# One more column group of the signal spectrum kept on chip, with a new order, new homes, banks and engines

## The chip, the cores and the metric

The kernel runs on one NeuronCore of a Trainium2 chip. The metric is the device time in microseconds of one execution of the whole program. An execution's time contains the profiled span and a little around it.

## The reference

Two independent parts share the kernel, each 2048 positions by 448 columns, and their outputs stand side by side. All data are bf16.

```python
# A: linear attention with a learned feature map, 16 heads of 28
pq, pk = q @ w_phi, k @ w_phi                  # per head
phi = concat(softmax(p), softmax(-p))          # for q and for k
kv, z = phi_k^T v, sum_s phi_k
a = ((phi_q kv) / (phi_q z + 1e-6)) @ wo
# B: a state-space convolution, 448 columns of 256 states
K[d, l] = Re sum_n C[d,n] exp(dt*A[d,n] * l) dt*B[d,n]
y = irfft(rfft(pad(u)) * rfft(pad(K)))[:2048] + u * Dskip
```

## The kernel before

**Part B** is a convolution by spectra. Its 448 columns are cut into eight chunks of 56 (112 with both halves of the states), and two chunks make one of four column groups (`GROUPS`). For each chunk: the *phases* are matmuls of a table of multiples with the log of the state's step (`dampings`, `rotations`); ACT makes exponentials and sines of them out of PSUM; DVE multiplies them (`damp`); a chain of five doublings (`hi_tables`) makes the coarse powers, each of two products and one addition; `build_k` multiplies the coarse and fine tables on PE into the kernel's values, which a copy brings from PSUM to SBUF. For each group: `scatter_k` moves these values by 36 small DMAs to the partitions where the transform wants them; `kernel_spectrum` transforms them on PE; `conv_group` multiplies the signal's spectrum `SU` and the kernel's spectrum `SK` on DVE, complex, as four big products of 3584 elements with three additions and some subtractions; `inverse` transforms back and stores.

The signal's spectrum is made early, for all groups, in `signal_spectrum`: 32 matmul blocks, each copied out of PSUM. The groups in `PARK` send theirs to DRAM (`SUd`) and read them back (`load_su`) before their convolution:

```python
if gi in PARK:
    sg = sb("sg", [128, 4, 112])
    copy(sg[:, :, :], (p, lambda t: t[:, :, :]))
    dma(["SP", "POOL"], SUd[gi][:, b, cp, st_, :, c0:c0 + 112], sg[:, :, :], ...)
else:
    copy(SUs[gi][:, b, cp, st_, :, c0:c0 + 112], (p, lambda t: t[:, :, :]))
```

**Part A** runs as 16 key tiles (projection, two exponentials, a DMA transpose, sums, one reciprocal, one product, accumulation in PSUM) and four query quarters (exponentials, reciprocals, four numerators, an addition of the two softmax halves, a transpose, the output projection and a store). Its tiles fill the gaps of part B.

**What sets the order.** The program first records 1366 units of work and runs none. Each unit lists the engines that may do it. `Plan.run` then issues them in the order of a table: each token of `ORDER` is a unit's number and the letter of its engine (P for PE, D for DVE, A for ACT, G for POOL, S for SP). Each engine keeps this order. `HOMES` gives every SBUF tile its byte address (one big tile `sbuf`, so all operands bear that name in the profile), and `BANKS` gives every PSUM tile its bank. A tile can lie where another one is done, and then waits for it.

Two kinds of unit can change engine with a meaning for this case. `copy` (L342) runs on ACT or DVE. An addition, `total`, runs on DVE (L379) or as a DMA issued by POOL that adds on the way (L381):

```python
if e == "DVE":
    nc.vector.tensor_tensor(out=dst, in0=dst, in1=t2, op=ALU.add)
else:
    nc.gpsimd.dma_start(out=view(dst), in_=view(t2), accum_op=ALU.add, ...)
```

Plain DMAs (L366) may go to SP or POOL, DMA transposes (L371) to SP. All matmuls are L351, products and subtractions on DVE L322, activations L332.

Of the kernel before, what the change touches and what calls it, by code (L numbers as in the profile page):

```python
# [30 lines left out]
PARK = [1, 2, 3]  # L31
# [60 lines left out]
0S 2A 3A 4S 5S 7S 28G 43P 44A 45D 42D 6S 46P 52A 49A 47P 30G 53D 71P 54A 72A 55D 73P 38G 51A 74A 50A 8S 140G 75P 77D  # L92
37S 48A 80D 76P 79D 17S 78D 57A 82D 56A 58D 81D 59D 649P 654A 61A 25S 657A 60A 655A 646P 648A 656A 39S 62D 650A 139G
141S 40S 69A 64A 142G 651A 143D 63D 144D 653A 95D 652A 88D 94D 89D 189S 190G 639P 19S 636P 65A 22S 41G 68A 191D 151P
647A 168P 640A 21S 18S 642A 638A 20S 118P 119A 225P 645A 226A 145P 637A 70D 169A 112P 192D 104D 210P 66D 23S 644A 24S
126P 643A 127A 641A 216P 211A 186P 102A 676D 113A 96G 180P 90G 219P 67D 92D 187A 217A 207P 114P 146A 218G 91D 97D 115A
93G 100A 122P 123A 213P 159P 98D 152A 214A 208A 103D 107A 680D 12S 124P 156P 116P 199P 234P 117A 200A 125A 34G 120P
675D 101D 235A 682D 677D 181A 121A 10S 9S 678D 681D 248P 105A 270P 272A 109D 259P 99G 660D 273A 262A 659D 171P 679D
201P 13S 220A 221G 250A 202A 195P 236G 196A 661D 174P 11S 170S 108D 261A 110A 172A 175A 106D 147P 212G 292P 294A 157A
303P 160A 295A 158G 183P 184A 658S 663D 662D 281P 283A 111D 237P 240A 14S 711D 148A 710D 712G 35G 203S 29G 165P 306A  # L100
664D 284A 166A 209G 239A 305A 149P 251A 204P 336P 150A 338A 153P 193P 188S 205A 194A 690P 154A 339A 665D 215G 666D
667D 669D 668D 670D 672D 671D 176S 696A 709S 714D 197P 687P 691A 155S 700P 673D 713D 688A 715D 27S 716D 693A 717D 198A
718D 297S 674G 685P 683P 689A 692A 695A 719D 694A 720D 708A 701A 707A 731D 721D 26S 1S 703A 161G 697P 698A 727D 699A
31G 725G 705A 173S 704A 314P 83P 722D 228P 206S 723D 684A 84A 129S 724G 686A 177P 702A 726D 229A 178A 179G 706A 85A
# [81 lines left out]
BANKS = "2246060577464565566424057205213025364344223317722252233000363614704367562041217134315736107506766202\  # L186
# [50 lines left out]
class Bytes:  # L237
# [32 lines left out]
def kernel(  # L270
# [752 lines left out]
    for gi, (c0, n) in enumerate(GROUPS):  # L1023
# [7 lines left out]
        scatter_k(gi, Ts)  # L1031
        if gi in PARK:
            load_su(gi)
# [33 lines left out]
```

## Time and profile before

| | before |
|---|---|
| median of 3 runs | 277.54 us (274.92 to 279.04) |
| the profiled execution | 275.77 us, span 274.0 us |
| PE busy | 233.8 us (85%) |
| DVE busy | 247.1 us (90%), 334 instructions |
| ACT busy | 235.0 us (86%), 414 instructions |
| POOL busy | 97.3 us (36%) |
| DMA moved | 39.10 MB |
| HBM read, written | 13.18 MB, 6.42 MB |

Busy time is time in which an engine works; neighbours on one engine overlap by about a tenth of a microsecond, so a group's busy time is less than its count by its mean. A group's line shows engine, operation, output and input with shapes, count, busy time, mean nanoseconds of one, and the engine's idle time just ahead with what ended it. The chain of waits follows the work that ended last back from the end. Three engines are almost equally full here, so a share of the span alone doesn't tell which of them sets the time; where one waits for another does.

### The profile page before, as it was taken

Reading aid. Unit: us, or ns where it says so; the run is one execution under the profiler, and the core shown is the slowest. Engines: PE = TensorE matmul, PEld = TensorE weight load, DVE = VectorE, ACT = ScalarE, POOL = GpSimd, SP = SyncE. Lnnn points to the kernel's source line nnn. Section 1 sums busy time; section 2 is a strip of 40 time slices with the busy share of each in tenths; the row PEclk is TensorE's granted clock in tenths of the full one; section 3 lists DMA queues with packets and bytes.
Section 4 is the critical chain, followed back from the end, with each engine's and each line's share of the span. In section 5 each row is a group of like instructions: output and inputs, shape, how many; then the busy total and the mean of one; then the engine's idle time right before and its main releaser. Section 6 shows DMA issues by size and latency. Waiting matters only on the chain.

```text
span 274.0 us, 10764 instructions
## 1 busy us (share of the span) xinstructions
PE 233.8 (85%) x4620; PEld 199.8 (73%) x4620; DVE 247.1 (90%) x334; ACT 235.0 (86%) x414; POOL 97.3 (36%) x169
## 2 busy tenths in 40 slices
PE   3825788999896797698999998979997998998994
PEld 3724686789786476376669977979895998788964
DVE  1699989999999899799899999997999989999891
ACT  3999999999999998996998999998969992756551
POOL 2400221260113330302942362176757210657450
PEclk9995999999999999999999999998999999999998
DMA  7996996455548797981431699399987797125764
GB/s 188 327 362 119 173 208 118 140 153 129 130 110 126 130 165 115 122 93 22 63 75 19 198 237 203 52 250 164 142 135 105 187 219 138 11 16 93 177 178 113
DMA packets 66969, 39.10 MB, mean 143 GB/s; under 512 B 53372, under 2 KB 62954, under 8 KB 66666
## 3 DMA queue, kind: packets, MB, share of 16 engines
q1 hardware_dynamic: 57914, 23.22, 40.7%
q0 software_dynamic: 8400, 14.94, 28.5%
q8 instruction: 36, 0.59, 1.0%
q10 hardware_dynamic: 608, 0.26, 0.3%
q14 instruction: 11, 0.09, 0.1%
HBM read 13.18 MB, written 6.42 MB: 72 GB/s over the span
## 4 chain that ended last, share of the span: by engine, by line
PE 31%; ACT 30%; DVE 19%; issue 8%; DMA 6%; SPq 4%; POOL 0%; ACTq 0%; DVEq 0%; POOLq 0%
PE psum L351 31%; ACT sbuf L332 20%; DVE sbuf L322 16%; ACT sbuf L342 5%; DMA sbuf<-sbuf 4%; SPq L366 4%; ACT L332 4%; ACT sbuf L337 1%; DVE sbuf L379 1%; DMA sbuf<-in_B_A_re_dram 1%; DVE sbuf L326 1%; DVE sbuf L545 0%; POOL sbuf L381 0%; DVE sbuf L342 0%; DVE sbuf L801 0%
## 5 line engine op out<-in xcount | busy, mean ns | idle before, releaser
L351 PE MATMUL psum<-sbuf 128*128 128x112 bf16 (+7 forms) x4620 | 233.8, 247 | 36.4 <-ACT sbuf L332 15.8
L351 PEld LDWEIGHTS <-sbuf 128*128 128x128 bf16 (+4 forms) x4620 | 199.8, 117 | 70.2 <-issue 38.5
L322 DVE TENSOR_TENSOR sbuf<-sbuf 128x896 bf16<-128x896 bf16 (+6 forms) x232 | 191.6, 873 | 13.8 <-ACT sbuf L332 9.2
L332 ACT ACTIVATE sbuf<-psum 128x448 bf16<-128x448 f32 (+4 forms) x221 | 138.5, 759 | 2.4 <-PE psum L351 2.0
L342 ACT CAST sbuf<-psum 128x448 bf16<-128x448 f32 (+3 forms) x167 | 84.1, 591 | 25.5 <-PE psum L351 25.0
L366 POOL DMA_DIRECT2D sbuf<-sbuf x68 | 46.8, 821 | 37.8 <-ACT sbuf L342 22.6
L381 POOL DMA_DIRECT2D sbuf<-sbuf x25 | 24.2, 994 | 66.1 <-DVE sbuf L322 47.4
L379 DVE TENSOR_TENSOR sbuf<-sbuf 128x896 bf16<-128x896 bf16 (+1 forms) x43 | 35.4, 833 | 0.4
L332 ACT ACT_TABLE_LOAD x17 | 21.8, 1283 | 5.0 <-PE psum L351 3.1
L366 POOL DMA_DIRECT2D out_dram<-sbuf x17 | 11.2, 693 | 17.0 <-ACT sbuf L342 17.0
L366 POOL DMA_DIRECT2D SUd<-sbuf x13 | 8.2, 649 | 23.8 <-ACT sbuf L342 23.8
L322 DVE TENSOR_TENSOR sbuf<-psum,sbuf 128x896 f32<-128x896 f32 (+4 forms) x14 | 8.8, 654 | 5.1 <-ACT sbuf L332 3.8
L731 POOL MEMSET sbuf<- 128x112 bf16 x16 | 3.7, 328 | 10.6 <-PE psum L351 10.4
L801 DVE RECIPROCAL sbuf<-psum 128x32 bf16<-128x32 f32 x16 | 5.3, 342 | 0.2 <-PE psum L351 0.2
L337 ACT CAST sbuf<-sbuf 128x1792 bf16<-128x1792 f32 x3 | 5.4, 1788 | 0.0
L337 ACT CAST sbuf<-psum 128x896 bf16<-128x896 f32 x2 | 1.8, 909 | 2.8 <-PE psum L351 2.8
L326 DVE SCALAR_TENSOR_TENSOR sbuf<-sbuf 128x64 f32<-128x64 f32 (+2 forms) x7 | 4.1, 590 | 0.0
L844 DVE RECIPROCAL sbuf<-psum 128x128 f32<-128x128 f32 x4 | 3.8, 949 | 0.2 <-PE psum L351 0.2
L366 POOL DMA_DIRECT2D sbuf<-SUd x2 | 1.7, 826 | 6.3 <-DVE sbuf L322 6.3
L342 DVE CAST sbuf<-psum 128x448 bf16<-128x448 f32 (+1 forms) x5 | 2.9, 583 | 0.9 <-PE psum L351 0.9
L332 ACT ACTIVATE sbuf<-sbuf 128x1792 f32<-128x1792 f32 x2 | 3.5, 1757 | 0.0
L847 DVE RECIPROCAL sbuf<-sbuf 128x64 f32<-128x64 f32 x4 | 2.1, 535 | 1.4 <-DMA sbuf<-sbuf 1.4
(21 smaller groups left out, 18.6 us busy)
## 6 DMA issues: line engine op xcount, KB each, us to landing
sbuf<-sbuf POOLq DMA_DIRECT2D x20, 224.0 KB, 4.9
sbuf<-sbuf POOLq DMA_DIRECT2D x8, 448.0 KB, 6.0
sbuf<-const SPq DMA_DIRECT2D x4, 640.0 KB
sbuf<-const SPq DMA_DIRECT2D x2, 1024.0 KB
out_dram<-sbuf POOLq DMA_DIRECT2D x17, 112.0 KB, 3.0
sbuf<-SUd SPq DMA_DIRECT2D x4, 448.0 KB
out_dram<-sbuf SPq DMA_DIRECT2D x15, 112.0 KB
SUd<-sbuf POOLq DMA_DIRECT2D x13, 112.0 KB, 2.7
```

Source lines behind the costliest of these rows:

```text
L322: lambda e: nc.vector.tensor_tensor(out=at(out_), in0=at(a), in1=at(b), op=op), [whose(a), whose(b)], [out_])
L326: lambda e: nc.vector.scalar_tensor_tensor(out=at(out_), in0=at(a), scalar=sc, in1=at(b), op0=op0, op1=op1),
L332: lambda e: nc.scalar.activation(at(out_), at(a), func, scale=scale, bias=bias), [whose(a)], [out_],
L337: plan.add({"ACT": 0.039 + sbuf + count(out_) * 0.8333e-3}, lambda e: nc.scalar.copy(at(out_), at(a)), [whose(a)], [out_])
L342: lambda e: (nc.scalar.copy if e == "ACT" else nc.vector.tensor_copy)(at(out_), at(a)), [whose(a)], [out_])
L351: nc.tensor.matmul(out_, lhsT=lhsT, rhs=rhs, start=start, stop=stop, **kw)
L366: plan.add({e: own[e] for e in engs}, lambda e: QUEUES[e].dma_start(out=out_, in_=in_, **kw), r, w, load=pieces / 16000 * max(11, 7.5 + 0. ...
L379: nc.vector.tensor_tensor(out=dst, in0=dst, in1=t2, op=ALU.add)
L381: nc.gpsimd.dma_start(out=view(dst), in_=view(t2), accum_op=ALU.add, max_dma_last_dim=3584)
L731: pool(0.5, lambda en: [nc.gpsimd.memset(w[:, c, ZERO, :], float(np.sqrt(0.5))) for c in range(2)], [], [w[:, 0, ZERO, :], w[:, 1, ZERO, :]])
L801: nc.vector.reciprocal(rk, pz.t)
L844: plan.add({"DVE": 0.868}, lambda e: nc.vector.reciprocal(rz[:, :, :, :], at(ndv(1))), [pz], [rz[:, :, :, :]])
```

## The change

`PARK` becomes `[2, 3]`: the second column group's signal spectrum (group 1) is written from PSUM straight into its tile in SBUF, where it stays until its convolution. Eight stores of 112 KB into DRAM and two loads of 448 KB leave the program, which has 1356 units now. `ORDER`, `HOMES` and `BANKS` are new throughout. No function changes.

```diff
-PARK = [1, 2, 3]
+PARK = [2, 3]
...
 ORDER = """
-0S 2A 3A 4S 5S 7S 28G 43P 44A 45D 42D 6S 46P 52A 49A 47P 30G 53D 71P 54A 72A 55D 73P 38G 51A 74A 50A 8S 140G 75P 77D
+666G 2A 42D 28G 0S 43P 44A 30G 5S 45D 71P 72A 3S 46P 52A 53D 4S 47P 54A 7S 55D 6S 73P 74A 49A 8S 140G 75P 80D 77D 76P
...
-BANKS = "2246060577464565566424057205213025364344223317722252233000363614704367562041217134315736107506766202\
+BANKS = "2023464076166131424510655700506365110224555076460201600227243512070746105235560102275202012037042042\
```

Counted over the whole table, what each engine is given:

| | before | after |
|---|---|---|
| copies out of PSUM: ACT, DVE | 167, 5 | 160, 12 |
| additions: DVE, POOL | 43, 25 | 39, 29 |
| plain DMAs: SP, POOL, ACT | 141, 106, 2 | 121, 117, 1 |
| DMA transposes: SP | 48 | 48 |
| ACT table loads | 17 | 17 |

Matmuls, activations and products are the same in number and size. Line numbers after are one lower than before.

Three places of the order. First DVE, in the damping of the sixth chunk (rows of 448, 1792 and 2688 elements, the last dimension 112), among the first query quarter's reciprocals and products. Before:

```order
L322 TENSOR_TENSOR sbuf<-sbuf 128x4x112 x2
L844 RECIPROCAL sbuf<-psum 128x128
L322 TENSOR_TENSOR sbuf<-sbuf 128x16x112
L322 TENSOR_TENSOR sbuf<-psum,sbuf 128x128
L322 TENSOR_TENSOR sbuf<-sbuf 128x1792 x2
L326 SCALAR_TENSOR_TENSOR sbuf<-sbuf 128x64
L322 TENSOR_TENSOR sbuf<-sbuf 128x2688
L847 RECIPROCAL sbuf<-sbuf 128x64
```

After:

```order
L321 TENSOR_TENSOR sbuf<-sbuf 128x4x112
L341 CAST sbuf<-psum 128x448
L321 TENSOR_TENSOR sbuf<-sbuf 128x896
L321 TENSOR_TENSOR sbuf<-sbuf 128x4x112
L843 RECIPROCAL sbuf<-psum 128x128
L341 CAST sbuf<-psum 128x448
L321 TENSOR_TENSOR sbuf<-sbuf 128x896
L321 TENSOR_TENSOR sbuf<-psum,sbuf 128x128
L321 TENSOR_TENSOR sbuf<-sbuf 128x4x112
L321 TENSOR_TENSOR sbuf<-sbuf 128x1792 x2
L341 CAST sbuf<-psum 128x2x224
```

Three copies out of PSUM (two query numerators and one of the first group's kernel spectrum) now stand in DVE's row, which before held none here.

Second POOL, from the additions of the query quarters to the first stores of results. `SUd_58` and `SUd_59` are the third and fourth group's parked spectrum before, `SUd_57` is the third group's after. Before:

```order
L381 DMA sbuf<-sbuf 128x2x448
L366 DMA sbuf<-sbuf 32x1x28
L366 DMA sbuf<-SUd_59 128x1792
L366 DMA sbuf<-SUd_58 128x1792
L381 DMA sbuf<-sbuf 128x1792
L731 MEMSET sbuf 128x112 x2
L366 DMA out_dram<-sbuf 512x1x112 x2
```

After:

```order
L380 DMA sbuf<-sbuf 128x1792
L365 DMA sbuf<-SUd_57 128x1792
L365 DMA sbuf<-sbuf 32x1x28
L365 DMA sbuf<-sbuf 4x1x28
L365 DMA sbuf<-in_A_wo_dram 64x1x448
L365 DMA sbuf<-sbuf 4x1x28
L365 DMA sbuf<-SUd_57 128x1792
L380 DMA sbuf<-sbuf 128x896
L365 DMA out_dram<-sbuf 512x1x112
L380 DMA sbuf<-sbuf 128x1792
L365 DMA sbuf<-sbuf 4x1x28
```

Both additions of the second group's convolution (128x1792) are DMAs now, and the second of them stands behind a store of the second group's first output half; between them is the eighth chunk's last table addition (128x896), which was on DVE.

Third DVE, from the end of the last damping to the third group's convolution: the addition of a query quarter (128x2x448) and what follows. Before:

```order
L379 TENSOR_TENSOR sbuf<-sbuf 128x2x448
L847 RECIPROCAL sbuf<-sbuf 128x64
L322 TENSOR_TENSOR sbuf<-sbuf 4x112
L322 TENSOR_TENSOR sbuf<-sbuf 128x3584
L379 TENSOR_TENSOR sbuf<-sbuf 128x1792
L379 TENSOR_TENSOR sbuf<-sbuf 128x896
L322 TENSOR_TENSOR sbuf<-sbuf 128x896 x3
```

After:

```order
L378 TENSOR_TENSOR sbuf<-sbuf 128x2x448
L321 TENSOR_TENSOR sbuf<-sbuf 128x3584
L341 CAST sbuf<-psum 128x49x7
L321 TENSOR_TENSOR sbuf<-sbuf 128x896 x2
L378 TENSOR_TENSOR sbuf<-sbuf 128x896
L321 TENSOR_TENSOR sbuf<-sbuf 128x896 x2
L378 TENSOR_TENSOR sbuf<-sbuf 128x896
L321 TENSOR_TENSOR sbuf<-sbuf 128x896
L341 CAST sbuf<-psum 128x448
```

The addition of 1792 elements is gone from here (POOL has it). The copy of one of the last two kernel builds (128x49x7), which ACT made before, stands behind the third group's first product (128x3584); the second of the two subtractions of 896 behind it is the second group's and needs both additions.

More of the change, by code (lines that the diff above doesn't have):

```diff
@@ L152 @@
-1180G 557A 616S 472G 1359D 1347A 558S 1348S 1360P 1363P 612S 1364A 1361D 1362S 1365S
-"""
-HOMES = {"PID": [62432], "H": [155776], "AT": [50432], "TH": [38592], "PW128": [42176], "PW256": [56704], "PW512":
-         [98720], "P64": [104608], "ident": [8384], "negid": [104096], "ones": [99168], "LT": [87552], "half":
-         [108576], "HZ": [34304], "IDX": [205600], "xT": [177376, 141792, 34944, 94848], "WpQ": [19072], "WpK":
[3 rows of a table removed]
-         "rawCre": [164352], "rawCim": [166528], "rawBre": [87680], "rawBim": [196576], "ldt": [141280], "dt":
[11 rows of a table removed]
-         12736, 99168, 50368, 173056], "EKT": [148640, 171200, 47552, 86176, 173056, 104352, 49536, 166528, 55808,
[3 rows of a table removed]
-         [22656, 99168, 177280, 56832, 34944, 170112, 70432, 82272], "oT_": [191680, 55808, 54784, 193280, 53760,
[9 rows of a table removed]
```

129 lines of the change are left out of this document (68 added, 61 removed), and 51 rows, old and new, of the table HOMES.

## The prediction

> **What bounds the kernel now.** I read the busy line first, then the chain of waits by engine, a table by stretches of the span, the groups by shape, the waits, and the chain in order of time.
>
> ```profile
> span 274.0 us, 10764 instructions
> PE 233.8 (85%) x4620; PEld 199.8 (73%) x4620; DVE 247.1 (90%) x334; ACT 235.0 (86%) x414; POOL 97.3 (36%) x169
> PE 31%; ACT 30%; DVE 19%; issue 8%; DMA 6%; SPq 4%; POOL 0%; ACTq 0%; DVEq 0%; POOLq 0%
> ```
>
> Three engines are nearly full and the chain passes between them; no queue of DMAs holds more than 4% of it. The table by stretches (us, then busy us and instructions of PE, weight loads, DVE, ACT, POOL, clock, DMA share, GB/s) says where each is fullest:
>
> ```profile
> 40.00:80.00 40.00, 36.64 (x714) 30.96 (x714) 39.01 (x52) 39.94 (x75) 9.31 (x20) 1.00 0.59 143
> 80.00:130.00 50.00, 41.04 (x953) 32.24 (x946) 47.05 (x71) 45.85 (x80) 11.32 (x21) 1.00 0.72 106
> 130.00:205.00 75.00, 71.52 (x1516) 62.37 (x1516) 70.83 (x107) 69.94 (x127) 39.05 (x62) 0.98 0.69 140
> 205.00:235.00 30.00, 26.97 (x582) 23.70 (x580) 28.31 (x40) 23.77 (x44) 9.19 (x16) 1.00 0.77 151
> 235.00:274.00 39.00, 33.75 (x532) 28.47 (x529) 31.45 (x40) 20.18 (x43) 19.77 (x33) 0.98 0.50 103
> ```
>
> From 40 to 80 ACT has no gap (0.06 us), from 130 to 205 PE idles 3.5 of 75. DVE idles 0.99, 2.95, 4.17 and 1.69 us in the first four stretches, 9.8 in all: that is all a better order can win on DVE between 40 and 235. Whom DVE waits for stands in the waits (us in total, times, longest) and in its first rows in order of time:
>
> ```profile
> DVE sbuf L322 <- ACT sbuf L332: 13.0, 11, 3.8
> ...
> PE psum L351 <- ACT sbuf L342: 4.4, 8, 0.9
> ...
> 3.16 0.63 DVE L322 TENSOR_TENSOR sbuf<-sbuf 112x448 bf16<-112x448 bf16 x1 [3.16 <-ACT sbuf L332]
> ...
> 7.71 2.09 DVE L322 TENSOR_TENSOR sbuf<-psum,sbuf 128x896 bf16<-128x896 f32 x2 [3.82 <-ACT sbuf L332]
> ...
> 36.45 4.10 DVE L322 TENSOR_TENSOR sbuf<-sbuf 128x1792 bf16<-128x1792 bf16 x4 [1.31 <-DMA sbuf<-sbuf]
> ```
>
> Of the 13.0 us behind ACT's exponentials and sines, 3.16 + 3.82 are the lead-in; 6.0 lie inside, at the start of the chunks' dampings. The chain in order of time shows the end:
>
> ```profile
> 217.55 2.63 ACT sbuf L332 x3
> ...
> 222.53 4.10 DVE sbuf L322 x4
> 226.63 0.55 DVE sbuf L379
> ...
> 227.22 4.73 PE psum L351 x152
> ...
> 235.41 0.70 SPq L366
> ...
> 247.40 3.49 DMA sbuf<-sbuf
> ...
> 251.03 2.73 PE psum L351 x52
> ...
> 254.40 2.04 DVE sbuf L322
> ...
> 270.27 0.53 ACT sbuf L342
> ```
>
> The last chunk's damping exponentials (217.55) let DVE finish the damping (to 226.63) and add up the last table (0.55); then come the last two kernel builds on PE, their scatter on SP (235.41 to 247.40), the last kernel spectrum, the last convolution (254.40) and the inverse. Whatever makes those exponentials end earlier moves all of this, if DVE keeps up.
>
> **The change part by part.** The rows by shape (busy us, mean ns, idle before):
>
> ```profile
> L342 ACT CAST sbuf<-psum 128x448 bf16<-128x448 f32 x147 | 75.0, 599 | 16.4 <-PE psum L351 15.9
> L322 DVE TENSOR_TENSOR sbuf<-sbuf 128x1792 bf16<-128x1792 bf16 x68 | 71.8, 1083 | 4.2 <-ACT sbuf L332 2.0 <-DMA sbuf<-sbuf 1.3 <-ACT sbuf L342 0.3
> L322 DVE TENSOR_TENSOR sbuf<-sbuf 128x896 bf16<-128x896 bf16 x88 | 50.6, 612 | 0.4
> L322 DVE TENSOR_TENSOR sbuf<-sbuf 128x2688 bf16<-128x2688 bf16 x16 | 24.7, 1554 | 0.6
> L322 DVE TENSOR_TENSOR sbuf<-sbuf 128x3584 bf16<-128x3584 bf16 x12 | 24.1, 2016 | 1.4 <-ACT sbuf L342 1.3
> L381 POOL DMA_DIRECT2D sbuf<-sbuf x25 | 24.2, 994 | 66.1 <-DVE sbuf L322 47.4 <-ACT sbuf L332 9.8 <-PE psum L351 5.2
> L379 DVE TENSOR_TENSOR sbuf<-sbuf 128x1792 bf16<-128x1792 bf16 x20 | 21.5, 1080 | 0.3
> L379 DVE TENSOR_TENSOR sbuf<-sbuf 128x896 bf16<-128x896 bf16 x23 | 14.2, 619 | 0.2
> L322 DVE TENSOR_TENSOR sbuf<-sbuf 128x448 bf16<-128x448 bf16 x32 | 11.5, 381 | 4.0 <-ACT sbuf L332 4.0
> L366 POOL DMA_DIRECT2D SUd<-sbuf x13 | 8.2, 649 | 23.8 <-ACT sbuf L342 23.8
> L342 DVE CAST sbuf<-psum 128x448 bf16<-128x448 f32 x3 | 1.9, 620 | 0.9 <-PE psum L351 0.9
> ```
>
> *Parking removed.* Eight stores of 112 KB and two loads of 448 KB go: ten issues on SP and POOL. POOL's ran 649 ns, behind waits of 23.8 us for ACT's copies, and POOL has 0% of the chain; SP's share lies in the last scatter alone, where no parking stands. The copies out of PSUM stay (they now write the resident tile), so no engine work goes. I take 0: cover is POOL at 36%. Were a load of the parked group what its convolution waited for, it would gain; but those products' whole group (128x3584) waited 1.4 us, for copies. Bounds: -1.3 to 0.
>
> *Engines chosen anew.* Net seven copies of 448 columns go from ACT to DVE (eleven copies go there and four come back; one each way is of 343 columns), and net four additions go from DVE to a DMA that adds, issued by POOL (three of 1792, one of 896 elements). ACT: -7 x 0.599 = -4.2 us. DVE: 7 x 0.620 - 3 x 1.080 - 0.619 = +0.5 us. PE's matmuls are the same. So DVE's own work, the largest, is not less.
>
> *ACT's lighter queue.* Seven copies fewer stand ahead of what DVE waits for. Bounds: 0, and the 6.0 us that DVE waits inside (4.0 in the row of 448 elements, 2.0 in that of 1792). Those waits can't shrink by more than ACT gets earlier, 4.2; nearly all of the seven stand ahead of the last damping or ease the queue up to it. I take -4.0, the end nearest to the 4.2 of the rows.
>
> *Copies in DVE's queue.* A copy waits in order for its matmul, with everything on DVE behind it. The order shows three such in the damping of the sixth chunk; behind them products and reciprocals of the query stage are queued, and the copies and transposes of those quarters wait for them. The trace has three such copies of 448 columns, which waited 0.9 us together, all of it at the last of them. For the ten moved in: 0 to 9; I take +0.5, near to the two that didn't wait, since DVE is behind PE through most of the span.
>
> *Additions moved to POOL.* The DMA rows (median us from issue to landing):
>
> ```profile
> sbuf<-sbuf POOLq DMA_DIRECT2D x20, 224.0 KB, 4.9
> sbuf<-sbuf POOLq DMA_DIRECT2D x8, 448.0 KB, 6.0
> ```
>
> The last table's addition leaves the chain (0.55 at 226.63). Its DMA is queued on POOL behind a load of parked spectrum, and six dampings are on DVE behind its products (two each of 448, 1792 and 2688 elements: 2 x 0.38 + 2 x 1.08 + 2 x 1.55 = 6.0 us) against 4.9: covered, gain at most 0.55. The second column group's addition is worse placed. In the changed order both halves are DMAs and the second stands on POOL behind an output store that waits for an ACT copy eleven instructions past the last damping exponential. Eleven at 0.51 (75.0 over 147) are 5.6; plus 0.65 for the store's issue and 6.0 to land: 12.3 us after that exponential. DVE asks for it after five dampings (5.6), a product of 3584, a multiplication of 1792, an addition and a subtraction of 896, and two small ones put at 0.9 (2.0 + 1.1 + 0.6 + 0.6 + 0.9 = 5.2): at 10.8. It would wait 1.5, with the third group's finishing steps, the reciprocals of the last query quarter and the third group's second products queued behind, and PE's inverse matmuls waiting for those. What idle DVE has between 226.6 and 254.4 (1.3 us in the 128x3584 row, behind copies) would take up part. Bounds 0 to +4 (an addition's landing took up to 8.5 us, below); I take +1.0.
>
> The Trainium skill's page "DMA: Bandwidth & Descriptors", section "Anatomy of one DMA", fits a POOL-issued transfer as 2.0 us plus bytes over 436 GB/s. For 448 KB that makes 3.1, an estimate by that page, where this trace has 6.0; by it the wait vanishes and the sum would be -3.0. The measured row decides.
>
> *The early additions.* The chain has this at the first state tables:
>
> ```profile
> 27.30 0.67 POOL sbuf L381
> 27.97 8.46 DMA sbuf<-sbuf
> ```
>
> DVE waited 1.31 us for it at 36.45. In the new order there stand between the product and its use two signal sums of 1792 and one operation of 1.08 us fewer, and two dampings of 448 and one of 1792 more: -2 x 1.08 - 1.08 + 2 x 0.38 + 1.08 = -1.4 us of cover, so the wait grows by 1.4. It lies ahead of the stretch where ACT is full, and DVE's chunks wait for ACT behind it; I take 0, and +1.4 if ACT's lead makes DVE the late one there.
>
> *Scatter and end.* SP still issues 18 and POOL 14 transfers into the last kernel tile: 0. The last stores are reordered: 0, -0.5 to +0.8. Homes and banks make waits that this trace can't show: bounds -1 to +2 (the largest waits inside for a buffer or a bank, PE behind ACT's copies, were 0.9 each), taken at 0.
>
> **Sum.** +0.5 - 4.0 + 0.5 + 1.0 = -2.0 us. Against the profiled execution, 275.77 us (span 274.0 and 1.77 around it), that is 273.8. That execution lies 1.77 under the median of the runs, 277.54, which spread from 274.92 to 279.04; against the median the forecast is **275.5**.
>
> **Rivals.** *A, the order closes most gaps.* Of DVE's 9.8 us idle between 40 and 235 some 80% go: -7.8 + 0.5 = -7.3, so 270.2. For it: the gaps are many and small. Against it: three engines are at 85 to 90%, so each gap closed on one must fit two others.
>
> *B, PE holds the middle.* From 130 to 205 PE idles 3.5 us in 75, with the same matmuls after. An ACT that is ahead then only waits, and just what is won before 130 can stay: DVE's 2.95 of idle from 80 to 130, of which I give a third. 277.54 - 1.0 + 0.5 + 0.5 + 1.0 = 278.5. Against it: PE enters that stretch when ACT lets it, so it may start it earlier.
>
> *C, slower: DVE waits in its own queue for PSUM.* Each of the ten copies moved in waits as the one at the end did, 0.9 us, instead of near 0. Half of that, 0.5 each, gives 277.54 + 0.5 - 4.0 + 5 + 1.0 = 280.0; all of it 284.0. It turns the change slower from 0.25 us each. For it: the order puts three of them right in a damping. Against it: ACT's copies as a group waited 15.9 us for PE over 147, 0.1 each.
>
> *D, slower POOL.* Fifteen more DMAs are issued by POOL, 20 fewer by SP. The additions took 994 ns each on POOL with DVE 90% busy. The Trainium skill's page "SBUF — State Buffer", section "Who interferes with whom", says that POOL can be locked out from writing descriptors while DVE holds the port that they share, and gives about 3.1 us in place of 0.62 for such a DMA. As a mechanism here: the addition before the third group lands two us later, the wait above is 3.5 and not 1.5: 277.5. The 994 ns speak against more.
>
> **How the numbers follow.** Chances: forecast 0.36, A 0.20, B 0.24, C 0.14, D 0.06. 2% is 5.5 us, about what a measurement can tell here. Faster by more: A and a little of the forecast's low side, 0.22. Slower by more (over 283.1): the upper half of C and the worst of the homes' waits, 0.11. Within: 0.67. The range goes from just under A, 269.5, to between C's two values, 282.0.
>
> **What would show it.** Right: copies on ACT down by 4 us, DVE's busy time within 1 us of 247.1, its waits behind ACT's exponentials well under 13.0, the last scatter starting some 2 us before 235. B: PE still near 95% from 130 to 205 and ACT with new waits for PE there. C: waits of DVE copies for PE of over 3 us in all. The addition: a DVE wait for a DMA of 1 to 2 us shortly after the last damping. Wrong in kind: a wait for a parked load, or a new one of several us in the first 40.

## The result and the profile after

The changed kernel takes 293.23 us (median; 291.49 to 301.18), beside 277.08 us of the kernel before on the same chip: a ratio of 1.056, 95% interval 1.045 to 1.068. It is slower by 16 us, where 275.5 was forecast and the range ended at 282.0. The profiled execution took 291.49 us, span 289.6. (Some executions are disturbed and longer; the ratios and, below, the median times of the experiments leave these out.)

First the busy line and the chain by engine, from the page of the kernel after:

```profile
span 289.6 us, 10761 instructions
PE 234.6 (81%) x4620; PEld 199.2 (69%) x4620; DVE 247.4 (85%) x337; ACT 233.1 (80%) x407; POOL 107.5 (37%) x184
PE 28%; ACT 13%; DVE 13%; issue 7%; DMA 6%; SPq 2%; POOL 0%; DVEq 0%; ACTq 0%; POOLq 0%
```

The three engines do the same work as before: PE +0.8 us, DVE +0.3, ACT -1.9. So the 15.6 us more of span are idle time on all three. Next, how much each engine worked in the first 40 us, as the sums of ten stretches of 4 us. Before:

```profile
sum 40.00, PE 23.89 PEld 22.05 DVE 30.42 ACT 35.35 POOL 8.66; mean PE 2.39 PEld 2.20 DVE 3.04 ACT 3.54 POOL 0.87
```

After:

```profile
sum 40.00, PE 17.55 PEld 16.29 DVE 21.04 ACT 28.92 POOL 5.96; mean PE 1.75 PEld 1.63 DVE 2.10 ACT 2.89 POOL 0.60
```

DVE is 9.4 us behind, PE and ACT 6.3 and 6.4, before the first chunk is done. DVE's instructions in order of time show where it stood still (start, us, what, in brackets the idle time ahead and what ended it). Before:

```profile
16.09 3.02 DVE L322 TENSOR_TENSOR sbuf<-sbuf 128x1792 bf16<-128x1792 f32 x2
...
22.57 9.03 DVE L322 TENSOR_TENSOR sbuf<-sbuf 128x1792 bf16<-128x1792 bf16 x8
```

After:

```profile
16.63 1.08 DVE L325 SCALAR_TENSOR_TENSOR sbuf<-sbuf 128x896 bf16<-128x896 f32 x1
27.95 5.96 DVE L321 TENSOR_TENSOR sbuf<-sbuf 128x1792 bf16<-128x1792 bf16 x4 [10.24 <-DMA sbuf<-in_B_u_dram,sbuf]
```

After, the sums of the signal's second half stand at the head of DVE's row, and they need a gathered (indirect) load that is late. Before, the products of the first sine tables (`cs16`, `cs48`) and their like stand there. The load itself is in the groups of DMA issues (last number: median us from issue to landing). Before:

```profile
sbuf<-in_B_u_dram,sbuf POOLq DMA_INDIRECT x2, 9.0
```

After:

```profile
sbuf<-in_B_u_dram,sbuf POOLq DMA_INDIRECT x2, 17.1
```

PE has the same fault, and passes it on to ACT. PE's matmuls in order of time, before:

```profile
15.23 0.95 PE L351 MATMUL psum<-sbuf 128*128 128x112 bf16 x16 [0.66 <-DVE sbuf L322]
23.91 4.14 PE L351 MATMUL psum<-sbuf 128*128 128x112 bf16 x52 [7.73 <-ACT sbuf L332]
```

After:

```profile
13.77 1.73 PE L350 MATMUL psum<-sbuf 128*128 128x112 bf16 x32 [1.01 <-DVE sbuf L321]
30.10 6.08 PE L350 MATMUL psum<-sbuf 128*128 128x112 bf16 x93 [14.60 <-DVE sbuf L321]
```

ACT's first damping exponentials (896 elements wide before, 448 after), before:

```profile
27.60 2.16 ACT L332 ACTIVATE sbuf<-psum 128x896 bf16<-128x896 f32 x3
```

After:

```profile
27.99 1.28 ACT L331 ACT_TABLE_LOAD   x1
33.93 0.98 ACT L331 ACTIVATE sbuf<-psum 128x448 bf16<-128x448 f32 x2 [4.66 <-PE psum L350]
```

After, PE made two blocks of the rotations' phases (32 matmuls from 13.77) and then stood for 14.60 us: the first signal blocks are next in its row, and the first damping's phases, which need only the early tables, are behind them. Before, PE stood here too, for 7.73 us, but for ACT, which was at work all that time; after, ACT itself runs dry. Its first damping exponentials start at 33.93 instead of 27.60.

Does the early delay reach the end? The table follows six steps that both kernels have, in us from the span's start (found by their units in each engine's row). The last two columns are experiments, below.

| | before | after | rows moved (e2) | also homes (e3) |
|---|---|---|---|---|
| ACT's first damping exponentials | 27.6 | 33.9 | 28.7 | 29.2 |
| first doubling's last product ends | 27.7 | 40.5 | 31.5 | 27.7 |
| second chunk's damping ends | 79.2 | 91.4 | 82.9 | 83.3 |
| eighth chunk's damping ends | 226.6 | 239.4 | 231.8 | 233.8 |
| last kernel build ends | 234.0 | 246.7 | 238.4 | 240.6 |
| last group's first product | 254.4 | 269.3 | 262.1 | 262.8 |
| span | 274.0 | 289.6 | 282.4 | 283.0 |

It does: 12.8 us at 40, 12.2 at 91, 12.7 at 247, then 2.9 more behind the last build.

### The profile page after: what moved, and what is told of

Its sections match the earlier page's. It is cut to its first block, busy times and chain, and to the rows that moved or that the text cites. A ratio compares the mean times of both kernels' runs of the same rounds, so it can differ in the third digit from the quotient of the medians.

```text
span 289.6 us, 10761 instructions
## 1 busy us (share of the span) xinstructions
PE 234.6 (81%) x4620; PEld 199.2 (69%) x4620; DVE 247.4 (85%) x337; ACT 233.1 (80%) x407; POOL 107.5 (37%) x184
## 4 chain that ended last, share of the span: by engine, by line
PE 28%; ACT 13%; DVE 13%; issue 7%; DMA 6%; SPq 2%; POOL 0%; DVEq 0%; ACTq 0%; POOLq 0%
PE psum L350 28%; DVE sbuf L321 11%; ACT sbuf L331 9%; DMA sbuf<-sbuf 6%; ACT sbuf L341 3%; SPq L370 2%; ACT L331 1%; DVE sbuf L843 1%; DVE sbuf L341 0%; DVE sbuf L378 0%; POOL sbuf L365 0%; DVE sbuf L846 0%; DVE sbuf L800 0%; DVE sbuf L325 0%; DVEq L321 0%
## 5 line engine op out<-in xcount | busy, mean ns | idle before, releaser
L350 PE MATMUL psum<-sbuf 128*128 128x112 bf16 (+7 forms) x4620 | 234.6, 247 | 51.1 <-DVE sbuf L321 17.1
L321 DVE TENSOR_TENSOR sbuf<-sbuf 128x896 bf16<-128x896 bf16 (+9 forms) x232 | 190.9, 875 | 20.5 <-DMA sbuf<-in_B_u_dram,sbuf 10.2
L341 ACT CAST sbuf<-psum 128x448 bf16<-128x448 f32 (+3 forms) x160 | 81.9, 601 | 30.2 <-PE psum L350 28.3
L380 POOL DMA_DIRECT2D sbuf<-sbuf x29 | 27.9, 973 | 97.2 <-DVE sbuf L321 50.7
L365 POOL DMA_DIRECT2D sbuf<-sbuf x72 | 49.4, 775 | 22.1 <-ACT sbuf L341 15.4
L378 DVE TENSOR_TENSOR sbuf<-sbuf 128x896 bf16<-128x896 bf16 (+1 forms) x39 | 31.7, 818 | 0.5
L365 POOL DMA_DIRECT2D out_dram<-sbuf x23 | 16.1, 773 | 20.0 <-ACT sbuf L341 17.6
L365 POOL DMA_DIRECT2D SUd<-sbuf x11 | 7.2, 715 | 16.0 <-ACT sbuf L341 16.0
L341 DVE CAST sbuf<-psum 128x448 bf16<-128x448 f32 (+1 forms) x12 | 7.2, 603 | 3.9 <-PE psum L350 3.9
L336 ACT COPY sbuf<-psum 128x896 f32<-128x896 f32 x2 | 1.8, 905 | 4.5 <-PE psum L350 4.5
L636 POOL COPY sbuf<-sbuf 1x2 bf16<-1x2 bf16 x6 | 0.9, 174 | 7.5 <-DMA sbuf<-in_B_A_re_dram 4.2
L365 POOL DMA_DIRECT2D sbuf<-const x4 | 3.2, 802 | 0.0
```

Source lines behind the costliest of these rows:

```text
L321: lambda e: nc.vector.tensor_tensor(out=at(out_), in0=at(a), in1=at(b), op=op), [whose(a), whose(b)], [out_])
L336: plan.add({"ACT": 0.039 + sbuf + count(out_) * 0.8333e-3}, lambda e: nc.scalar.copy(at(out_), at(a)), [whose(a)], [out_])
L341: lambda e: (nc.scalar.copy if e == "ACT" else nc.vector.tensor_copy)(at(out_), at(a)), [whose(a)], [out_])
L350: nc.tensor.matmul(out_, lhsT=lhsT, rhs=rhs, start=start, stop=stop, **kw)
L365: plan.add({e: own[e] for e in engs}, lambda e: QUEUES[e].dma_start(out=out_, in_=in_, **kw), r, w, load=pieces / 16000 * max(11, 7.5 + 0. ...
```

## The experiments

Theories. *The rows*: work that needs the late load stands ahead of work that doesn't, on DVE, PE and ACT. *The landing*: the load is late because of what is issued ahead of it. *The homes*: tables wait for addresses that the signal's tiles still hold. *The engines and the tail*: the new engines of copies and additions, and more work behind the last build. *The parking*: keeping the spectrum in SBUF is itself a loss or a gain. Edits of the order are shown as one engine's row; a token is a unit.

**e1_loads: the load of the first half ahead of the weight transposes.** 185 and 141 on SP are the direct loads of the two halves, 17 to 20 the transposes of part A's weights, 25 a table.

```diff
 SP   185S
-25S 18S 20S 141S 19S 17S
+25S 141S 18S 20S 19S 17S
```

> The changed kernel with one edit in SP's row alone: the two transposes of weights that stand ahead of the load of the first signal half now stand behind it. Theory L (the gathered load lands 17.0 us after its issue, 9.0 before, because the transposes' small packets run beside it): it lands about 9 us after its issue, near 20.3 us, DVE's wait for it falls from 10.2 to 2 to 3 us, and the time falls by about 7, to 286. Theory L wrong about the transposes: the landing stays at 17 us and the time at 293. Theory T (the loss is the added copies and additions later in the rows, and the early wait is made up for): 293 in either case.

Measured: 295.22 us, 1.072 (1.060 to 1.084). The gathered loads (the rows of their tile: from issue to landing) landed no sooner, and DVE waited as in the kernel after:

```profile
DMA to landing us min/median/max: 17.2/18.1/19.0
...
28.14 4.03 DVE L321 TENSOR_TENSOR sbuf<-sbuf 128x1792 bf16<-128x1792 bf16 x3 [10.46 <-DMA sbuf<-in_B_u_dram,sbuf]
```

So this place on SP is not what delays them.

**e2_rows: nothing waits behind the load.** On DVE the sums of the second half (188, 187) go behind the products of the first sine tables (62, 58, 63, 59); on PE two signal blocks (217, 201) behind the first damping's phases; the copy of one block likewise on ACT.

```diff
 DVE  82D
-188D 187D 62D 58D 63D 95D 94D 59D 144D
+62D 58D 63D 59D 188D 187D 95D 94D 144D
 PE   641P 638P
-217P 201P 631P 628P
+631P 628P 217P 201P
```

> The changed kernel, loads as they are; in DVE's row the two sums of the second signal half stand behind the sine and cosine products of cs48 and cs16, and in PE's row the first two signal blocks stand behind the phases of the first chunk's damping (ACT's copy of the first block with them). Theory R (the loss comes from what stands behind the waiting sums and blocks in the rows of DVE and PE): DVE does 4 to 5 us of products while it waits, PE's phases go at 16 and ACT's damping exponentials no longer wait until 33.9; the first doublings (H16) end 4 to 6 us earlier and the time is 287 to 289. The landing stays at 28. Theory T: 293.

Measured: 283.88 and 284.33 us in two executions, too few for a ratio; the profiled one has 7.2 us less span than after (289.6 to 282.4). DVE no longer waits for the load, although that still takes 13 us from issue to landing (17.1 after; why it came 4 us sooner, with no DMA moved, isn't known):

```profile
DMA to landing us min/median/max: 12.8/13.0/13.1
...
23.25 10.17 DVE L321 TENSOR_TENSOR sbuf<-sbuf 128x1792 bf16<-128x1792 bf16 x9
```

**e3_homes: the first doubling waits for no sum.** The table `H` lies where after has the second half's tiles; its products (95, 94, 89, 88) can't run ahead of the sums. On top of e2: two free homes for these tiles, and the products go ahead.

```diff
-"ua": [94880, 160640], "ub": [53248, 149792]
+"ua": [94880, 104384], "ub": [53248, 205600]
 DVE  62D 58D 63D 59D
-188D 187D 95D 94D 144D 143D 89D 88D
+95D 94D 89D 88D 188D 187D 144D 143D
```

> As e2_rows, and the second half's two signal loads have homes of their own (104384 and 205600), so that the table H no longer lies on them and its four products (4.3 us) go ahead of the sums as well. Theory R: nothing that DVE has to do before 28 waits for the load, its wait for the gathered load is under 2 us, the first doublings end near where they did before the change (28 to 30), and the time falls by 9 to 11, to 282 to 284, although the load still lands at 28. Theory L alone (the landing itself is what costs): no better than e2_rows. Theory T: 293.

Measured: 284.11 us, 1.025 (1.014 to 1.036): clear of after's interval, 3.1 points or some 8.5 us less. But beside e2's two executions the homes add nothing: the first doubling ends where it did before the change (27.7), and at the second chunk's damping nothing is left of that (83.3, in e2 82.9). Of PE's 14.60 us behind the sums, 10.90 remain as a wait for ACT:

```profile
26.33 3.15 PE L350 MATMUL psum<-sbuf 128*128 128x112 bf16 x32 [10.90 <-ACT sbuf L331]
```

The phases wait for PSUM banks that ACT still reads. (Before, one of their two blocks had free banks at 15.2, and the other waited 7.73 us.) This wait costs ACT nothing: it works on without a gap until the exponentials, from 29.2.

**e4_all: e3 and e1 together.** On top of e3:

```diff
 SP   185S
-25S 18S 20S 141S 19S 17S
+25S 141S 18S 20S 19S 17S
```

> e3_homes and e1_loads together. Theory R and L: with the rows and homes eased the landing is covered, so the earlier landing adds at most 1 to 2 us: 281 to 283, what is left over the time before (277.1) being the later part of the loss, 3 to 4 us behind the last damping. Theory L alone: 286, as e1_loads.

Measured: 281.69 us in one execution, which doesn't tell it from e3 (282.76 to 285.1). The profile is of another execution, of 293.8 us: there the load landed after 21.7 us, and DVE waited 4.8 us for it again. So the moved rows cover a landing of 13 us, not one of 22.

**e5_loadrow: all loads of the first 45 us in the order of before.** SP's and POOL's rows, on top of e3 (also the load of C_re, 5, third in SP's row, and 666 further back in POOL's):

```diff
 SP   37S
-1S 185S 25S 18S 20S 141S 19S 17S 39S 40S 10S
+17S 25S 39S 141S 40S 185S 19S 18S 20S 10S 1S
 POOL
-666G 28G 30G 140G 139G 186G 38G 142G 96G 90G 41G
+28G 30G 38G 140G 139G 142G 186G 41G 96G 90G
```

> e3_homes, and the rows of SP and POOL up to about 45 us in the order that they had before the change: the first small load of weights early on POOL, one transpose ahead of the big tables, both signal halves and only then the other transposes; the two gathered loads one right behind the other. Theory L2 (a gathered load and the transposes slow each other when they run at once; before, the transposes queued behind both signal halves): the gathered loads land 8 to 11 us after their issue (13 to 14.5 in e2_rows and e3_homes), SP's transposes are issued without stalls of 7 us, and the time is 280 to 283. If it is the place of the transposes that counts and not the homes, e1 and e4 got worse because they put four in one piece beside the gathers. Theory L2 wrong: landing 13 and more, time 284 to 285.

Measured: 283.91 us, 1.030 (1.023 to 1.037); the loads land in 8.3 and 11.1 us. No faster than e3: with the rows mended, landing earlier gains nothing that these runs can tell.

**e7_before_turns: the transposes moved early in the kernel before.**

```diff
 SP   37S 17S 25S
-39S 141S 40S 189S 19S 22S 21S 18S 20S
+19S 18S 20S 39S 141S 40S 189S 22S 21S
```

> The kernel before the change with one edit: three of the weight transposes, which stood behind both signal halves in SP's row, stand ahead of them. Theory L2: they now run beside the gathered loads, which land 13 us or more after their issue (7.6 and 10.4 before), DVE, which asks for them at 21 to 23, waits 2 to 6 us, and the time rises by as much, to 279 to 283. Theory L2 wrong: landing under 11, 277.

Measured: 283.5 us, 1.024 (1.013 to 1.034). The gathers landed as before (7.7 and 10.4 us), so transposes ahead do not by themselves make them late. Another DMA was late: the first state table's additions, issued by POOL from 29.30 on, for which DVE waited until 43.05 (the slowest took 8.5 us from issue to landing before, 13.1 here).

```profile
29.30 1.83 POOL L381 DMA_DIRECT2D sbuf<-sbuf  x2 [15.68 <-ACT sbuf L332]
...
43.05 6.41 DVE L322 TENSOR_TENSOR sbuf<-sbuf 128x1792 bf16<-128x1792 bf16 x7 [5.90 <-DMA sbuf<-sbuf]
```

Before, this row of DVE starts at 36.45. It is 6.6 us late here, the second chunk's damping 7.0 (86.2 for 79.2), the end 8.1 (span 282.1 for 274.0). Three DMAs moved in an otherwise unchanged kernel cost 6 to 7 us: a delay in the first 40 us does reach the end.

**e6_head and e8_engines: the first 160 units in the order of before, on all engines, with e3's homes; then also the 23 copies and additions on the engines of before.**

```diff
 ORDER (all engines)
-the first 160 units as after has them
+the same units as before has them, then the rest as after
```

> The changed kernel with the homes of e3_homes and the first 160 units of the table (up to some 45 us) on every engine in the order of before, as far as the new homes and banks let them; the rest of the table, the engines and the straight copies of the second group's spectrum are those of the change. Theory H (the loss of the change is in its first 45 us): the first doublings end near 28 and the first chunk's damping near 50, the time is 275 to 279, the same as before. Rival (the later rows lose too): some 4 us over before at the second chunk's damping already, and 282 to 285 in the end, as e3_homes.

> e6_head with the 23 copies and additions that changed their engine back on the engine that they had before (ACT 167 copies, DVE 5; DVE 43 additions, POOL 25); order and homes as in e6_head. The forecast's terms (ACT lighter by 4.2 us and worth 4.0; copies in DVE's row +0.5; DVE +0.5; an addition on POOL +1.0) make it 2.0 slower than e6_head. Rival (the moved copies wait on DVE, the additions land late): 2 to 4 faster than e6_head.

Measured: 305.5 us, 1.102 (1.089 to 1.115), and 302.77 us, 1.100 (1.094 to 1.107). Both far slower: the seam between two orders made ACT's first damping exponentials end at 62.5 us. They say nothing on the head as a whole; against each other they compare the engines (below).

**e10_head2, e14_head3, e16_head4: the lead-in still closer to before.** On top of e5: e10 gives the first damping's phases two free banks and reorders ACT's and DVE's first sines, exponentials and products; e14 also loads the table C_re first; e16 also puts two steps of DVE in the table ahead of an exponential of ACT (no engine's row changes, only the order in which the table is read).

```diff
 ACT (e10)   57A
-645A 61A 60A 647A 68A 649A 56A
+56A 61A 60A 645A 647A 68A 649A
 DVE (e10)   82D
-62D 58D 63D 59D
+58D 59D 62D 63D
 SP (e14)   0S
-3S 4S 5S
+5S 3S 4S
 table (e16)
-52A 47P 54A 73P 74A 49A 30G 53D 55D
+52A 53D 47P 54A 55D 73P 74A 49A 30G
```

> e5_loadrow with three further edits in the first 35 us: the first phases of the first damping get two PSUM banks that are free at 15 (they had those of the rotations' phases, which ACT reads until 28), the first two signal blocks get these in exchange, and in ACT's row the exponentials and sines of the two small tables stand ahead of the rotations' sines, with DVE's products of them in the same order. Theory B (banks and ACT's row, not the loads, make what is left of the early loss in e5_loadrow): DVE's 8.1 us wait for ACT goes, PE's 8.8 us wait for ACT goes, the second chunk's damping ends 2 to 4 us earlier, and the time is 280 to 282 (283.9 in e5_loadrow). Rival: the early part is made good already and all that is left comes later: 283 to 284.

> e10_head2 with one transfer moved: the load of C's real part goes first again in SP's row, as in the changed kernel (in e5_loadrow and e10_head2 it came third, PE's first transposes waited for it and DVE started its first product at 11.8 in place of 7.7). Theory S (that lost the 3 to 4 us which the edits of e10_head2 had won): DVE's longest wait for ACT falls from 8.2 to 4.2 and the time from 285.5 to 281 to 282.5. Rival (the rows behind 40 us give nothing back for an earlier start): 284 to 285.

> e14_head3 with DVE's first two products ahead of ACT's first small exponential in the table: in e5_loadrow to e15_head3_eng they stood behind it and DVE began them at 11.3 to 11.8 in place of 7.2 to 7.7. Theory S2 (this, not the load of C's real part, ate what those edits had won): DVE's longest wait for ACT falls from 7.8 to 4, the second chunk's damping ends within 1 us of where it did before the change (79.2), and the time falls from 285.9 to 281 to 282.5. Rival (the rows behind 40 us give nothing back for an earlier start): 284 to 286.

Measured: 285.45 us, 1.031 (1.022 to 1.041); 285.72 us, 1.026 (1.018 to 1.035); 285.14 us, 1.031 (1.020 to 1.041). None gains on e5. From e5 to e14 DVE's first big product waits for ACT. e14:

```profile
11.25 2.09 DVE L319 TENSOR_TENSOR sbuf<-psum,sbuf 128x896 bf16<-128x896 f32 x2 [7.75 <-ACT sbuf L329]
```

After:

```profile
7.67 2.09 DVE L321 TENSOR_TENSOR sbuf<-psum,sbuf 128x896 bf16<-128x896 f32 x2 [4.22 <-ACT sbuf L336]
```

e16 took the added part of that wait away, and nothing came of it. The profiles of e15 and e17 below, which differ in this alone, show where it goes: the first big product starts at 11.35 and 7.54, the first doubling's last product ends at 28.2 and 26.0, the second chunk's damping at 83.0 and 83.3. A start 4 us earlier is gone by then.

**e11_engines, e15_head3_eng, e17_head4_eng: the engines of before.** Each adds to e5, e14 and e16 the change of e8: 23 copies and additions go back.

```diff
-862A 387D 897G 1020G 900D 310D  ...
+862D 387A 897D 1020D 900G 310A  ...
```

> e5_loadrow with the 23 copies and additions that changed their engine back on the engine that they had before the change; nothing else. By the forecast's terms (ACT lighter 4.0, copies on DVE -0.5, DVE's work -0.5, an addition on POOL -1.0) 2.0 slower than e5_loadrow, 286. Rival (ACT is ahead and only waits, as PE holds the middle; the moved copies and additions cost): 0 to 3 faster, 281 to 284.

> e14_head3 with the 23 copies and additions back on their engines of before. As e11_engines against e5_loadrow (2.1 faster, in intervals that overlap): 279 to 280.5. If that difference was chance: as e14_head3 within 1. What it is then still over before (277.5) belongs to the order behind 45 us and to the straight copies.

> e16_head4 with the 23 copies and additions back on their engines of before. In two of three pairs so far the engines of before were about 2 us faster, in the third (e15_head3_eng against e14_head3) not to be told. Engines of the change cost 1 to 2: 279 to 281. They cost nothing: as e16_head4 within 1. They are worth the 2.0 of the forecast: 283 to 284.5.

Measured: 281.77 us, 1.017 (1.008 to 1.026); 283.92 us, 1.026 (1.019 to 1.033); 283.29 us, 1.025 (1.020 to 1.031). Beside their partners the ratio falls by 1.29, 0.01 and 0.51 points, and by 0.22 from e6 to e8. The new engines came out faster in none of the four pairs; they cost 0 to 1.3 points, 1.4 us in the mean, each pair within its intervals. e11 is the best of all versions and still slower than the kernel before.

**e12_cut: less work for PE at the end.** Two query quarters' output projections take one matmul of four (their output is then only a quarter of the sum).

```diff
-mm(t[:, :], oT_[:, k, :], wo[:, k, :], k == 0, k == 3) for k in range(4)
+mm(t[:, :], oT_[:, k, :], wo[:, k, :], k == 0, k == NK - 1) for k in range(NK)   # NK = 1 if sc < 2 else 4
```

> The changed kernel with work left out: the output projections of the first two query quarters (eight, seven of them behind the last kernel build on PE) make one of their four matmuls. Theory P (behind the last kernel build PE works without a gap, 36.8 us against 34.9 before, and sets the end): 21 matmuls of some 0.2 us fewer, the time falls by 3.5 to 4.5 us, to 289. Rival (the convolutions on DVE or the scatter's landing set the end, PE only fills): less than 1 us, 292 to 293.

The stretch from the last build to the end (us; busy us and instructions of PE, weight loads, DVE, ACT, POOL; clock, DMA share, GB/s). Before:

```profile
233.90:274.00 40.10, 34.85 (x537) 29.06 (x536) 32.55 (x42) 21.19 (x45) 19.94 (x33) 0.98 0.48 101
```

After:

```profile
246.60:289.60 43.00, 36.75 (x578) 30.27 (x576) 33.15 (x45) 19.79 (x41) 20.21 (x34) 0.99 0.48 104
```

e12:

```profile
245.50:287.60 42.10, 34.71 (x552) 29.62 (x550) 33.35 (x45) 19.24 (x41) 20.25 (x34) 0.96 0.52 104
```

After has 41 more matmuls of PE here, 1.9 us, and 2.9 us more time. (By the order, 40 of them are the last query quarter's 32 sums, one numerator and one output projection.) e12 takes 2.0 us of PE work out and 0.9 us of time; 292.23 us in all, 1.060 (1.050 to 1.071), so the rival came out and not theory P. PE's extra work is at most a part of the tail's 2.9 us.

**e9_park, e13_park2, e18_park3: the second group parked again.** After with the eight stores and two loads put back, in three placings: as first written; with POOL's first store behind the additions; and with SP's store behind the transposes too.

```diff
-PARK = [2, 3]
+PARK = [1, 2, 3]
 SP (e9, e13)   10S
+206S
 21S 24S 23S 22S
 POOL (e9)   93G
+209G
 99G
+161G
```

> The changed kernel with the parking of the second group put back and nothing else: its eight copies go to the same addresses as before the edit but are stored to DRAM from there (four stores on SP, four on POOL) and loaded back into them by two loads on SP ahead of the group's products, as far ahead in the rows as they stood before the change; all other units, homes, banks and engines are those of the changed kernel. The forecast's term (parking worth 0, bounds 0 to 1.3): 293 to 294.5. Rival (the straight copies themselves cost something): under 291.5. Rival (parking had cost several us that the rest of the change gave away again): 296 or more.

> As e9_park, with the parked stores on POOL moved behind the four additions of the first doublings, so that none of these stands behind a store that waits for its copy. Theory Q (the 15 us of e9_park were the additions queued on POOL behind such a store, not the traffic): the 10.6 us wait of DVE for an addition goes, and the time is 293 to 295, parking by itself being worth 0 to 1.3 as forecast. Rival (the traffic or the issues cost wherever they stand): 298 and more.

> As e13_park2, with two stores moved: in e9_park and e13_park2 a parked store on SP waited some 16 us for its copy out of PSUM, and four weight transposes and two of the input stood behind it in SP's row (issued at 46 to 48 in place of 31). Here that store stands behind these transposes, and one store on POOL behind the next one. Theory Q2 (the 15 us were this queueing, not the traffic): the transposes go at 31 again, and the time is 292 to 295, parking itself worth 0 to 1.3 as forecast. Rival (parking's traffic costs where two transfers meet, as e.g. the added loads with the last scatter): 297 and more.

Measured: 308.69 us, 1.117 (1.106 to 1.127); 308.59 us, 1.107 (1.098 to 1.116); 304.85 us, 1.106 (1.098 to 1.113). Theories Q and Q2 named times of 292 to 295 and fell as such. In e9 the store stands on SP until its copy is made, and the transposes with it. After:

```profile
31.30 5.15 SPq L370 DMA_TRANSPOSE sbuf<-in_A_wqkv_dram  x4
```

e9:

```profile
47.27 0.36 SPq L363 DMA_DIRECT2D SUd<-sbuf  x1
47.68 6.10 SPq L368 DMA_TRANSPOSE sbuf<-in_A_wqkv_dram  x4
...
91.97 2.10 DVE L319 TENSOR_TENSOR sbuf<-sbuf 128x1792 bf16<-128x1792 bf16 x2 [10.65 <-DMA sbuf<-sbuf]
```

e13 moved other stores than the one that DVE's wait hung on: there it still waited 9.48 us for this addition, and SP's stall stayed. In e18 the transposes are back at 31.9, but the same happens on POOL. After:

```profile
66.32 0.54 POOL L365 DMA_DIRECT2D SUd<-sbuf  x1 [2.11 <-ACT sbuf L341]
66.86 0.90 POOL L380 DMA_DIRECT2D sbuf<-sbuf  x1
```

e18:

```profile
77.30 1.07 POOL L363 DMA_DIRECT2D SUd<-sbuf  x2 [11.61 <-ACT sbuf L339]
78.36 0.90 POOL L378 DMA_DIRECT2D sbuf<-sbuf  x1
...
85.56 2.09 DVE L319 TENSOR_TENSOR sbuf<-sbuf 128x1792 bf16<-128x1792 bf16 x2 [10.90 <-DMA sbuf<-sbuf]
```

A store waited 11.61 us for ACT's copy, the table addition behind it went out 11.5 us later, DVE waited 10.90, and the span is 11.9 longer than after's. These figures fit the price of a bad place in a queue; no run has the stores well placed, so what parking itself costs stays open.

## Why the prediction was wrong

**The step that failed** is one that the sum didn't have: where the signal's loads, sums and first blocks stand in the in-order rows of the first 40 us. The sum's only place for new waits was "Homes and banks make waits that this trace can't show: bounds -1 to +2 [...], taken at 0", and it wasn't homes (e3 gains nothing over e2). Under "The early additions" the text even saw that two signal sums had moved, and counted them as cover alone, not whether their own load has landed. At the end it named the case ("a new one of several us in the first 40") and gave it no price. The wait measured 10.24 us on DVE, 14.60 on PE (7.73 before) and 4.66 on ACT; moving the rows (e2) took 7.2 us of span back, nearly half of the 15.6. Part of it was to be had from before's trace and the new order: before's gathers are issued at 9.7 and 11.0 us and the slower takes 10.4 to land. With after's issue at 10.96 that is 21.4, and DVE comes to the sums at 17.7: a wait of 3.7 us. The other 6.5 are the later landing.

Two more terms were mis-sized. "The last stores are reordered: 0, -0.5 to +0.8": behind the last build the span grew by 2.9 us, past these bounds, and no cause is shown for it. The other is the next.

**ACT's lighter queue, -4.0.** Here a mechanism failed. Seven copies did leave ACT, but its busy time fell by 1.9 us, not 4.2. Of the waits of DVE behind ACT's exponentials inside the kernel, before (us in total, times, longest):

```profile
DVE sbuf L322 <- ACT sbuf L332: 6.1, 9, 1.2
...
DVE sbuf L847 <- DMA sbuf<-sbuf: 1.4, 1, 1.4
```

After:

```profile
DVE sbuf L321 <- ACT sbuf L331: 5.6, 8, 1.2
...
DVE sbuf L325 <- DMA sbuf<-sbuf: 3.5, 1, 3.5
...
DVE sbuf L341 <- PE psum L350: 0.6, 2, 0.3
```

These waits shrank by 0.5 us, and an upper bound had been taken as the value. Why an ACT that is lighter doesn't help shows at the last chunk's sines, for which ACT first loads a table (`ACT_TABLE_LOAD`). e14, with the engines of the change:

```profile
211.21 1.28 ACT L329 ACT_TABLE_LOAD   x1 [6.26 <-issue]
```

e15, with those of before:

```profile
210.38 1.28 ACT L329 ACT_TABLE_LOAD   x1 [2.70 <-issue]
```

In e14 ACT is there 2.7 us earlier (at 204.95, in e15 at 207.68) and only waits longer: the sines need phases from PE, and in PE's row both kernel builds of the seventh chunk, which PE begins at 202.7 and 202.9, stand ahead of them. In after the wait is 5.56 us, before 2.16. So what the seven copies gave ACT was waited away at this place.

The second rows are two different waits in the query quarters. The one after is a small operation (128x64) whose inputs are made on DVE ahead of it, so it can only wait for the address of its output. That address (163360) lies within the span of the table `H` (158048 to 169248) that a DMA is reading for the last chunk: a home, then, though no run moved it. With before's engines it waits 0.5 us (e15) and 0.7 (e17) instead of 4.0 (e14) and 3.9 (e5).

**DVE's own work, +0.5,** was right: +0.3. **Copies in DVE's queue, +0.5,** came to 0.6 up to the last build: that is what all copies on DVE waited for PE until then (last row above). Over the whole kernel the ten copies of 448 columns waited 3.9 us, so rival C's sign (over 3 us) came true:

```profile
L341 DVE CAST sbuf<-psum 128x448 bf16<-128x448 f32 x10 | 6.1, 615 | 3.9 <-PE psum L350 3.9
```

Its mechanism didn't: 3.3 of the 3.9 lie behind the last build, 2.26 of them at one copy 4 us before the end, and the three copies in the sixth chunk's damping waited 0.3 together.

**Additions moved to POOL, +1.0.** The second group's addition, issued at 223.7, made nobody wait: 0. After's groups have for the additions on POOL (busy us, mean ns):

```profile
L380 POOL DMA_DIRECT2D sbuf<-sbuf x29 | 27.9, 973 | 97.2 <-DVE sbuf L321 50.7 <-DVE sbuf L544 22.4 <-DVE sbuf L800 10.7
```

And its DMA issues (KB each, median us to landing):

```profile
sbuf<-sbuf POOLq DMA_DIRECT2D x11, 448.0 KB, 5.7
```

As in the trace of before, an addition holds POOL for some 1 us (973 ns), so D's mechanism did not appear. The 3.1 us that D took from the Trainium skill's "SBUF — State Buffer" stand there in the section "A bandwidth-pool intuition that's wrong (but worth ruling out)" and are told of a DMA beside a `tensor_copy` on DVE; DVE's work here is mostly products and additions (`TENSOR_TENSOR`).

The 448 KB land in 5.7 us. By the fit in the Trainium skill's "DMA: Bandwidth & Descriptors", section "Anatomy of one DMA", it would be an estimated 3.1; the measured row decides.

**Parking removed, 0,** is neither shown nor refuted. Its reason, "cover is POOL at 36%", is refuted as a way of reasoning: POOL is busy 37% after, and in e18, where a store on POOL waited 11.61 us, DVE waited 10.90 for the addition behind it.

**Rivals A and B.** A fell with the result. B's condition was a full PE from 130 to 205; in the matching stretch after, PE has gaps:

```profile
140.00:217.00 77.00, 69.80 (x1505) 60.20 (x1505) 72.14 (x111) 70.48 (x123) 40.37 (x63) 0.98 0.68 131
```

69.80 of 77 is 91%, before 95%. So B's condition isn't met over the stretch. But what it said of ACT, "An ACT that is ahead then only waits", is what e14 and e15 show at the last chunk's sines, with PE as the one waited for (PE itself had waited 2.56 us for a DMA there in e14, before it began the two builds). Its time, 278.5, fell too.

**What stays open.** e3, e5 and their kind remain 2.5 to 3% (7 to 8 us) slower. By the table, 4 us of e3's are there by 83 us, 7 by 234, 9 at the end: they come in small pieces, of which the engines are about 1.4. Of the first 4, some 2.5 are work: from 30 us to the end of the second chunk's damping DVE is busy 50.2 us in e3 and 47.7 before, as the new order puts more ahead of that point. No single cause was found for the rest. Which of the early waits, DVE's or PE's, sets the end wasn't separated, as e2 moves both rows. Nor was it found why the gather lands late.

## What to carry to other kernels

When an order is searched anew, read each in-order engine's first rows against the landing times of the loads they need, before adding up any savings: one instruction at the head of a row that waits for a late load stops everything behind it, and in a kernel as full as this one little of it was won back (12.8 us at 40, 12.7 at 247). A low busy share of a queue that issues DMAs is no cover; what counts is how long the instruction ahead waits. And a bound ("can't shrink by more than ACT gets earlier, 4.2") isn't a value: take it only where the row shows the wait that it would remove, and ask what the relieved engine waits for next.

## What the runs showed of the hardware

The same gathered load took between 8 and 22 us from issue to landing: 7.6 and 10.4 us before, 17.1 after, 21.7 in the profile of e4, 8.3 and 11.1 in e5. In the packets of after's trace from 16 to 20 us, those of the gather (7168 bytes) took 597 ns in the mean, against 276 before in the same stretch, and those of 256 bytes, as the weight transposes have them, 139 against 83. That fits a crowding of transposes and gather, but e7 put three of the transposes ahead and the gather stayed at 7.7 to 10.4, so it is not shown. The slowest 448 KB addition of the first 60 us took 8.5 us before and 13.1 in e7.

After PE had stood for a while its granted clock was lower, and its first matmuls took longer. After (start and end, us; busy us and matmuls of PE, then weight loads, DVE, ACT, POOL; clock, DMA share, GB/s):

```profile
28.00:32.00 4.00, 1.90 (x21) 1.90 (x21) 4.00 (x4) 1.27 (x1) 0.00 (x0) 0.50 0.46 43
32.00:36.00 4.00, 4.00 (x75) 3.97 (x73) 4.00 (x4) 2.07 (x5) 0.00 (x0) 0.90 0.46 91
```

The wait of 14.60 us ends at 30.10. Up to 32 us, 21 matmuls (128x112) took 1.90 us, some 90 ns each, at a clock of 0.50; in the next 4 us it was 53 ns each, at 0.90. The trace of before has the same behind its wait of 7.73 us (52 matmuls from 24 to 28 us, 77 ns each, at 0.65). So this isn't a part of the difference: PE's busy time was 233.8 us before and 234.6 after.
